# Tile 2 of a layer's token tiles in seven half-depth products of 256 tokens

## The chip, the cores and the metric

One core of a Trainium2 chip runs the program. The time of a run is what the device takes for one execution, in microseconds (us); a kernel's time is the median of its runs. The engines are TensorE (PE in the profile; its weight loads are PEld), VectorE (DVE), ScalarE (ACT) and GpSimd (POOL); SyncE (SP) issues the DMAs. Each engine takes its instructions in the order in which the program has them, and waits on semaphores where one needs what another engine wrote, or writes where another has still to read.

## What is computed

A retention layer over 2 batches of 768 tokens (8 heads of 64) gives x of 1536 tokens by 512. Two feed-forward layers follow, each 512 to 2048 to 512:

```python
def _moe_ref(x, w_in, w_out):
    h = x @ w_in
    g = np.maximum(h, 0.0) + np.log1p(np.exp(-np.abs(h)))
    return (g @ w_out).astype(np.float32)

def _moe2_ref(x, w_in, w_out, s, b):
    h = x @ w_in
    r = np.maximum(h, 0.0)
    g = s * (r * r) + b
    return (g @ w_out).astype(np.float32)
```

## The kernel before, in words

Tokens lie in three tiles of 512 (0, 1 and 2), the 2048 hidden units in 16 blocks of 128, in layer two taken as 8 pairs. The weights come as 64-bit numbers and are decoded on the chip (`split_w`: three VectorE steps and a ScalarE step make `wm`). Every operand of a product is kept in two parts, hi (`xh`, `wh`, `gh`) and lo (`xl`, `wl`, `gl`), and a product is three: hi by hi, hi by lo, lo by hi. ScalarE writes the hi part, GpSimd the lo part as the difference (`split`, L110 to L115; `parts_x`, L474).

The first matrix product of a layer takes a contraction of 512. `all_of` (L495) does it for one tile and block in 12 products of 512 columns. For tiles 0 and 1 of a pair together, the function `second` (L943) uses a scheme with seven products of half depth instead of eight: the 2 by 2 blocks are the halves of the contraction, the two weight blocks and the two tiles. Each of the seven is six products (`six`, L487). They use four sums of weights (`sums_w`, L306, on GpSimd; split into `sh`, `sl` by `split_sums`) and four sums of x (`sum_x`, L435; split into x1 to x4 once). Part results are kept by ScalarE copies out of the bank (`kept`, L502: p1, p5, u2) and added by VectorE (`joined`, L513). A product that adds on to a bank must come after the copy of what was there. The first pair of a layer goes without the scheme (`plain`, L915). Tile 2 is done by `all_of`, two times 12 products.

`begin`, `middle` and `finish` make g out of h: in layer two a relu out of the bank, a square, a scale with shift, and the hi part, all on ScalarE, then the lo part on GpSimd. The second matrix product is `acc_2` (12 products per tile and block); `take_2` (L580) brings its four banks to SBUF (`xa`) by four VectorE instructions of 512 columns, copies in the first pair, sums later.

The order is written out by hand. A pair in `second` has six slots. `part` starts the decode of one half of the next weights, `go_first` and `go_last` (L859 to L864) do steps of it ahead of and behind the second matrix product of the pair before, and `end_part` does its last step, the split. `pair` (L607) gives the order of the halves of a pair: (w, 0), (w + 1, 0), sums (w, 2), (w, 1), split of the sums (w, 3), (w + 1, 1). `load_w` (L269) issues the load of a half from SP into one of four buffers (`raw`); the decode of each half issues the load of a later one.

Layer two starts with `plain(1, 0, ...)` (L1068), in whose slots `all_x` makes the sums of x and `parts_x` splits them; then come seven pairs by `second`, and the last second products with the output.

Of the kernel before, what the change touches and what calls it, by code (L numbers as in the profile page):

```python
# [13 lines left out]
P = 128  # L14
# [34 lines left out]
def tile_retention_mlps(ctx: ExitStack, tc: tile.TileContext, head, w1, w2, sb, out):  # L49
    nc = tc.nc  # L50

    cp = ctx.enter_context(tc.tile_pool(name="cp", bufs=1))
    rawp = ctx.enter_context(tc.tile_pool(name="raw", bufs=4))
    dp = ctx.enter_context(tc.tile_pool(name="dec", bufs=2))
# [214 lines left out]
    def load_w(w, i):  # L269
        layer, f = divmod(w, NF)  # L270
        t = rawp.tile([P, DM, 2], U32, tag="raw", name="raw")
        nc.sync.dma_start(out=t.rearrange("p a b -> p (a b)"), in_=(w1, w2)[layer][f, :, i].bitcast(U32))
        raw_t[w, i] = t

    def split_w(w, i):
# [17 lines left out]
        nc.scalar.activation(m, hw.bitcast(F32), AF.Copy, scale=REBIAS)  # L293
        load_next()
        yield
# [205 lines left out]

    def kept(ps, tag):  # L502
        t = late.tile([P, TT], F32, tag=tag, name=tag)
        nc.scalar.activation(t, ps, AF.Copy)
        return t

    turn = [0]
# [5 lines left out]
    def joined(ps, t, here=False):  # L513
        c = ps if here else next_t()
        nc.vector.tensor_tensor(out=c, in0=ps, in1=t, op=ALU.add)  # L515
        return c
# [105 lines left out]
    at[1, PAIRS] = len(halves)  # L622
    RAWS = 4
# [92 lines left out]
    with tc.manual_schedule():  # L716
# [141 lines left out]

        def go_first():  # L859
            if work not in sums_of_w:  # L860
                go(work, 2)
# [81 lines left out]
        def second(la, p):  # L943
# [12 lines left out]

            part(base + 2)
            six(one, a11, b11, True)
# [3 lines left out]
            end_part()  # L962
            go_first()
# [5 lines left out]
            part(base + 3)  # L969
            six(other, s1, t1, True)  # L970
# [3 lines left out]
            end_part()  # L974
            go_first()
            whole(*of_pair(la, p - 1, 1, 1))
            go_last()

            part(base + 4)
            six(other, s4, b22, False)  # L980
# [3 lines left out]
            end_part()  # L984
            go_first()
            middle(c12)
# [5 lines left out]

            part(base + 5)
            six(one, a22, x_t[4], False)
            c21 = begin(la, one, tags=("u2", "p1"))
            end_part()
            go_first()
            whole(*of_pair(la, p - 1, 2, 1))
# [3 lines left out]

            part(base + 6)
            all_of(third, (ah, al), 2)
            ha = begin(la, third)
            end_part()
            go_first()
            middle(ha)
# [3 lines left out]

            part(base + 7)
# [4 lines left out]
            go_first()  # L1018
            middle(hb)
# [3 lines left out]
            finish(la, p, 1, 2, hb)  # L1023
            go_last()

        def all_x():
# [142 lines left out]
```

## Time and profile before

| | |
|---|---|
| runs | 567.87, 565.83, 565.73 us; median 565.83 |
| span of the profiled execution, from its first to its last instruction | 564.1 us |
| around the span, against the median | 1.7 us |
| TensorE busy | 559.1 us (99%), 2972 products |
| weight loads of TensorE busy | 461.8 us (82%) |
| VectorE busy | 368.0 us (65%) |
| ScalarE busy | 339.4 us (60%) |
| GpSimd busy | 340.9 us (60%) |
| loads of raw weights | 64 of 512 KB, 3.6 us from issue to landing |

The profile is one execution of the program. Busy time is the time in which an engine works at something; the chain that ended last goes back from the last instruction, at each step to what released it. A row of a timeline has the start in us from the span's start, the duration, the engine, the line of the code and the operation, what it writes and reads, and in brackets the idle time of the engine before it with what ended it. The durations of neighbouring instructions of an engine overlap somewhat, so the step from start to start says what one costs.

### The profile page before, as it was taken

Reading aid. Unit: us, or ns where it says so; the run is one execution under the profiler, and the core shown is the slowest. Engines: PE = TensorE matmul, PEld = TensorE weight load, DVE = VectorE, ACT = ScalarE, POOL = GpSimd, SP = SyncE. Lnnn points to the kernel's source line nnn. Section 1 sums busy time; section 2 is a strip of 40 time slices with the busy share of each in tenths; the row PEclk is TensorE's granted clock in tenths of the full one; section 3 lists DMA queues with packets and bytes.
Section 4 is the critical chain, followed back from the end, with each engine's and each line's share of the span. In section 5 each row is a group of like instructions: output and inputs, shape, how many; then the busy total and the mean of one; then the engine's idle time right before and its main releaser. Section 6 shows DMA issues by size and latency. Waiting matters only on the chain.

```text
span 564.1 us, 8073 instructions
## 1 busy us (share of the span) xinstructions
PE 559.1 (99%) x2972; PEld 461.8 (82%) x2972; DVE 368.0 (65%) x556; ACT 339.4 (60%) x616; POOL 340.9 (60%) x289
## 2 busy tenths in 40 slices
PE   8999999999999999999999999999999999999997
PEld 7877888888888888888888888888888888888886
DVE  4887768776757759786859865645645646544224
ACT  3766673544555665543437797768585966766560
POOL 4457467776598797733525996556565646556130
PEclk9999999999999999999999999999999999999999
DMA  8996211101222213322212022222122121100005
GB/s 341 407 355 223 74 42 56 57 19 59 74 76 74 76 37 112 110 79 78 67 43 76 21 92 75 76 73 67 47 76 74 59 92 37 38 0 2 0 4 220
DMA packets 15014, 50.58 MB, mean 90 GB/s; under 512 B 1792, under 2 KB 2048, under 8 KB 14976
## 3 DMA queue, kind: packets, MB, share of 16 engines
q1 hardware_dynamic: 14976, 50.08, 25.4%
q8 instruction: 23, 0.38, 0.3%
q14 instruction: 15, 0.12, 0.1%
HBM read 46.93 MB, written 3.15 MB: 89 GB/s over the span
## 4 chain that ended last, share of the span: by engine, by line
PE 97%; DVE 1%; DMA 1%; ACT 0%; issue 0%; DVEq 0%
PE acc L576 35%; PE acc L400 12%; PE h L490 10%; PE h L349 8%; PE y L498 7%; PE third L498 7%; PE y L490 5%; PE y L349 4%; PE third L490 2%; PE y L191 2%; PE h L498 2%; PE s L172 2%; PE h L191 1%; DMA qk<-head 1%; PE acc L172 1%; PE acc L191 1%
## 5 line engine op out<-in xcount | busy, mean ns | idle before, releaser
L586 DVE TENSOR_TENSOR xa<-acc,xa 128x512 f32<-128x512 f32 x131 | 81.7, 684 | 98.3 <-PE acc L576 98.1
L115 POOL TENSOR_TENSOR gl<-c,gh 128x512 fp32r<-128x512 f32 x69 | 91.8, 1334 | 83.0 <-ACT gh L112 65.0
L115 POOL TENSOR_TENSOR wl<-wm,wh 128x512 fp32r<-128x512 f32 x64 | 83.8, 1309 | 93.9 <-ACT wh L112 93.8
L576 PE MATMUL acc<-wh,gh 128*128 128x512 f32 x190 | 74.1, 390 | 0.0
L576 PE MATMUL acc<-wh,gl 128*128 128x512 f32 x190 | 73.9, 389 | 0.0
L576 PE MATMUL acc<-wl,gh 128*128 128x512 f32 x190 | 51.7, 389 | 0.0
L112 ACT ACTIVATE gh<-c 128x512 fp32r<-128x512 f32 x69 | 43.6, 632 | 11.1 <-POOL c L550 7.0
L297 DVE SCALAR_TENSOR_TENSOR wm<-wm,cu,word 128x512 uint32<-128x512 uint32 x54 | 40.1, 742 | 12.3 <-ACT wm L293 11.5
L293 ACT ACTIVATE wm<-raw 128x512 f32<-128x512 f32 x64 | 42.1, 658 | 7.1 <-POOL wl L115 7.0
L576 PEld LDWEIGHTS acc<-wh,gh 128*128 128x128 f32 x190 | 35.7, 188 | 8.2 <-DVE xa L586 0.4
L290 DVE SCALAR_TENSOR_TENSOR word<-raw,cu,word 128x512 uint32<-128x512 uint32 x54 | 40.8, 756 | 1.9
L576 PEld LDWEIGHTS acc<-wl,gh 128*128 128x128 f32 x190 | 35.7, 188 | 7.5
L576 PEld LDWEIGHTS acc<-wh,gl 128*128 128x128 f32 x190 | 35.7, 188 | 7.3
L112 ACT ACTIVATE wh<-wm 128x512 fp32r<-128x512 f32 x64 | 39.7, 620 | 3.1 <-DVE wm L297 3.0
L548 ACT ACTIVATE c<-c,sbt 128x512 f32<-128x512 f32 x48 | 39.2, 817 | 1.6
L362 ACT ACTIVATE t<-t 128x512 f32<-128x512 f32 x24 | 15.1, 628 | 39.0 <-DVE t L356 39.0
L400 PE MATMUL acc<-gh,wh 128*128 128x512 f32 x96 | 37.9, 395 | 0.0
L522 ACT ACTIVATE c<-c 128x512 f32<-128x512 f32 x21 | 13.3, 632 | 40.5 <-DVE c L515 39.9
L400 PE MATMUL acc<-gl,wh 128*128 128x512 f32 x96 | 37.4, 390 | 0.0
L288 DVE TENSOR_SCALAR word<-raw 128x512 uint32<-128x512 uint32 x54 | 37.1, 687 | 0.5
L576 PE MATMUL acc<-gh,wh 128*128 128x512 f32 x96 | 37.3, 389 | 0.0
L576 PE MATMUL acc<-gl,wh 128*128 128x512 f32 x96 | 37.3, 389 | 0.0
(240 smaller groups left out, 1390.7 us busy)
## 6 DMA issues: line engine op xcount, KB each, us to landing
raw<-w SPq DMA_DIRECT2D x64, 512.0 KB, 3.6
qk<-head SPq DMA_DIRECT2D x12, 512.0 KB, 8.4
kv<-head SPq DMA_DIRECT2D x12, 512.0 KB, 8.4
out<-xa SPq DMA_DIRECT2D x11, 256.0 KB, 2.1
cst<-head SPq DMA_DIRECT2D x1, 518.0 KB, 4.5
cst<-head SPq DMA_DIRECT2D x1, 256.0 KB, 5.5
out<-xa SPq DMA_DIRECT2D x2, 128.0 KB, 1.8
sbt<-sb SPq DMA_DIRECT2D x1, 1.0 KB, 10.2
```

The costliest lines, as they stand in the source:

```text
L112: nc.scalar.activation(hi, src, AF.Copy)
L115: lo_eng.tensor_tensor(out=lo, in0=src, in1=hi.bitcast(F32), op=ALU.subtract)
L290: nc.vector.scalar_tensor_tensor(out=x, in0=hw, scalar=cu[:, 0:1], in1=x, op0=ALU.bitwise_and, op1=ALU.bitwise_or)
L293: nc.scalar.activation(m, hw.bitcast(F32), AF.Copy, scale=REBIAS)
L297: nc.vector.scalar_tensor_tensor(out=m.bitcast(U32), in0=m.bitcast(U32), scalar=cu[:, 1:2], in1=x, op0=ALU.logical_shift_left, op1=ALU.bit ...
L349: nc.tensor.matmul(ps, w[:, cc * P : (cc + 1) * P], r[j][:, cc, :], start=i == 0, stop=i == len(ops) - 1)
L400: nc.tensor.matmul(acc_t[la, g, j][cc], *ops[i], start=f4 == 0 and i == 0, stop=ends(s) and i == 2)
L490: nc.tensor.matmul(ps, w[a][:, k * P : (k + 1) * P], x[b][:, k], start=start and i == 0, stop=i == len(ops) - 1, skip_group_check=True,)
L498: nc.tensor.matmul(ps, w[a][:, k * P : (k + 1) * P], (xh, xl)[b][j][:, k], start=i == 0, stop=i == len(ops) - 1)
L548: nc.scalar.activation(c, c, AF.Identity, scale=sbt[:, 0:1], bias=sbt[:, 1:2])
L576: nc.tensor.matmul(acc_t[la, p, "pair", j][cc], *ops[i], start=half == 0 and i == 0, stop=half == 1 and i == 2)
L586: nc.vector.tensor_tensor(out=dst, in0=ps, in1=dst, op=ALU.add)
```

## The change

Tile 2 goes into the scheme as well, from the second pair of layer two on. Its 512 tokens are cut into two halves of 256 (`LEFT`, `RIGHT`), which play the part that tiles 0 and 1 play; the sums of weights are those of the pair already. `last_tile` replaces the last two slots of `second` in layer two: seven times six products of 256 columns, with copies and sums of 256 columns, among them the second products of tile 0 in halves of two banks (`FIRST`, `SECOND`).

The scheme needs four sums of x of tile 2, z1 to z4, made once (`sum_z`, `parts_z`): nine VectorE instructions of 512 elements over hi and lo parts, in `all_z` in the last two slots of `plain`, four hi parts on ScalarE and four lo parts on GpSimd; z4 is split in the last slot of `plain`, z1 to z3 in the first two slots of the first `second`. They live in `xa[2]`, and split in places of `xh`, `xl` that are free by then, z4 in buffers of its own. To make room for those the raw buffers of the weights become three, with a fourth in a pool that ends with the retention layer.

The sums of weights are needed to the end of a pair now. So their split moves to the last slot of the pair before, everything in the decode of layer two comes one slot later (`- la`), and the four GpSimd sums are done at the head of their slot (`go_first(la)`).

```diff
-    rawp = ctx.enter_context(tc.tile_pool(name="raw", bufs=4))
+    rawp = ctx.enter_context(tc.tile_pool(name="raw", bufs=3))
...
     def load_w(w, i):
         layer, f = divmod(w, NF)
-        t = rawp.tile([P, DM, 2], U32, tag="raw", name="raw")
+        k = halves.index((w, i))
+        pool, more = (rp, {"tag": "raw_"}) if k in FOURTH else (rawp, {"tag": "raw"})
+        t = pool.tile([P, DM, 2], U32, name="raw", **more)
...
-        load_next()
+        if halves.index((w, i)) != FOURTH[-1]:
+            load_next()
...
+    def room_z(k):
+
+        if k < 3:
+            return [wide(t[1][:, k - 1]) for t in (xh, xl)]
+        if k == 3:
+            return [t[2][:, 0:2, RIGHT] for t in (xh, xl)]
+        return [late.tile([P, 2, HT], F32R, tag=f"z{e}", name=f"z{e}") for e in "hl"]
+
+    def sum_z(ks):
+
+        def of(half, cols):
+            return [t[2][:, 2 * half : 2 * half + 2, cols].bitcast(F32) for t in (xh, xl)]
+
+        add, less = ALU.add, ALU.subtract
+        (h11, l11), (h12, l12), (h21, l21), (h22, l22) = (of(a, b) for a in (0, 1) for b in (LEFT, RIGHT))
+        z1, z2 = raw_z(1), raw_z(2)
+        todo = {
+            1: ((h12, h11, less), (None, l12, add), (None, l11, less)),
+            2: ((h22, z1, less), (None, l22, add)),
+            3: ((z2, h11, less), (None, l11, less)),
+            4: ((h21, z2, less), (None, l21, add)),
+        }
+        for k in ks:
+            for x, y, op in todo[k]:
+                nc.vector.tensor_tensor(out=raw_z(k), in0=raw_z(k) if x is None else x, in1=y, op=op)
+
+    def parts_z(k):
+        z_t[k] = hi, lo = room_z(k)
+        split(hi, lo, raw_z(k), nc.scalar, nc.gpsimd)
...
-            return [(w, 0), (w + 1, 0), (w, 2)] + [(w, 1), (w, 3)][:: 1 if la else -1] + [(w + 1, 1)]
+            return [(w, 0), (w + 1, 0), (w, 2)] + [[(w, 3), (w, 1), (w + 1, 1)], [(w, 1), (w + 1, 1), (w, 3)]][la]
...
+    FOURTH = 3, 7
...
-        def go_first():
-            if work not in sums_of_w:
+        def go_first(la):
+            if work not in sums_of_w or la and len(sums_of_w) % 2:
                 go(work, 2)
...
-            part(base + 2)
+            part(base + 2 - la)
...
+            if la and p == 1:
+                parts_z(1)
...
+            if la and p == 1:
+                parts_z(2)
+                parts_z(3)
...
+            if la:
+                last_tile(la, p, base, third, (a11, a12, a22), (s1, s2, s3, s4))
+                return
...
+        def last_tile(la, p, base, third, a, sums):
+
+            (a11, a12, a22), (s1, s2, s3, s4) = a, sums
+            q11, q21, q22 = (
+                [t[2][:, 2 * k : 2 * k + 2, cols] for t in (xh, xl)] for k, cols in ((0, LEFT), (1, LEFT), (1, RIGHT))
+            )
+            z1, z2, z3, z4 = (z_t[k] for k in (1, 2, 3, 4))
+
+            part(base + 6 - la)
+            other = bank(ps_y, "y")
+            u, v, w_, x = other[:, LEFT], other[:, RIGHT], third[:, LEFT], third[:, RIGHT]
+            six(u, a11, q11, True)
+            p1 = kept(u, "p1", HT)
+            six(w_, a12, q21, True)
+            six(x, s1, z1, True)
+            p5 = kept(x, "p5", HT)
+            joined(w_, p1, True)
+            end_part()
+            go_first(la)
+            acc_2(la, p, 0, 0, FIRST)
+            six(u, s2, z2, False)
+            u2 = kept(u, "u2", HT)
+            six(x, s4, q22, False)
+            joined(x, u2, True)
+            ha = begin(la, third)
+            acc_2(la, p, 0, 0, SECOND)
+            finish(la, p, 0, 2, ha)
+            go_last()
+
+            part(base + 7 - la)
+            six(u, s3, z3, False)
+            joined(u, p5, to=v)
+            end_part()
+            go_first(la)
+            acc_2(la, p, 0, 1, FIRST)
+            take_2(la, p, 0, FIRST)
+            six(u, a22, z4, False)
+            hb = begin(la, other)
+            acc_2(la, p, 0, 1, SECOND)
+            take_2(la, p, 0, SECOND)
+            finish(la, p, 1, 2, hb)
+            go_last()
+
+        def all_z():
+            sum_z((1, 2))
+            yield
+            sum_z((3, 4))
+            parts_z(4)
+            yield
...
-        plain(1, 0, left, [[sums_1], [sums_1], [], [sums_1], [], []], [(1,), (3, 2), (), (4,), (), ()])
+        sums_z = all_z()
+        plain(1, 0, left, [[sums_1], [sums_1], [], [sums_1], [sums_z], [sums_z]], [(1,), (3, 2), (), (4,), (), ()])
```

Where instructions stand now is seen best in the built programs. Lines of the changed kernel are shifted: L293 before is L295 now, L297 is L300, L481 is L484, L504 is L507, L515 is L558, L522, L547 and L548 are L565, L590 and L591. First ScalarE late in layer two's `plain`, before, from a split of weights to tile 2's relu, square, scale and hi part for the first block (`sh` is the hi part of the sums of weights, `x4h` that of x's fourth sum):

```order
L112 ACTIVATE wh_3184<-wm 128x512
L112 ACTIVATE sh<-ws 128x512 x2
L481 ACTIVATE x4h<-xa_110 128x1024
L522 ACTIVATE c<-third 128x512
L547 ACTIVATE c<-c 128x512
L548 ACTIVATE c<-c,sbt 128x512
L112 ACTIVATE gh<-c 128x512
```

The same stretch now:

```order
L112 ACTIVATE wh_3182<-wm 128x512
L295 ACTIVATE wm<-raw 128x512
L484 ACTIVATE x4h<-xa_110 128x1024
L565 ACTIVATE c<-third 128x512
L590 ACTIVATE c<-c 128x512
L591 ACTIVATE c<-c,sbt 128x512
L112 ACTIVATE gh<-c 128x512
L112 ACTIVATE wh_3229<-wm 128x512
L112 ACTIVATE sh<-ws 128x512 x2
```

A decode's `wm` stands where `sh` stood, and `sh` comes behind the tile and one more split.

Next ScalarE at the end of `plain`, before, up to the first copy of the first `second` pair (`p_3328<-h`; `c<-y` begins tile 2's second block):

```order
L522 ACTIVATE c<-y 128x512
L547 ACTIVATE c<-c 128x512
L548 ACTIVATE c<-c,sbt 128x512
L112 ACTIVATE gh<-c 128x512
L112 ACTIVATE wh_3279<-wm 128x512
L293 ACTIVATE wm<-raw 128x512
L504 ACTIVATE p_3328<-h 128x512
```

And now (`zh` is the hi part of z4, `p_3339<-h` the first copy):

```order
L565 ACTIVATE c<-y 128x512
L590 ACTIVATE c<-c 128x512
L591 ACTIVATE c<-c,sbt 128x512
L112 ACTIVATE gh<-c 128x512
L295 ACTIVATE wm<-raw 128x512
L112 ACTIVATE zh<-xa_111 128x512
L507 ACTIVATE p_3339<-h 128x512
```

`zh` has come between the last `wm` and the first copy.

VectorE at the same place, before, from tile 0's copies out of the banks (`xa_109<-acc`, L584) over two decodes to the join that reads the first copy:

```order
L584 COPY xa_109<-acc_3216 128x512 x2
L584 COPY xa_109<-acc_3217 128x512
L584 COPY xa_109<-acc_3218 128x512
L288 TENSOR_SCALAR word<-raw 128x512
L290 SCALAR_TENSOR_TENSOR word<-raw,cu,word 128x512
L297 SCALAR_TENSOR_TENSOR wm<-wm,cu,word 128x512
L288 TENSOR_SCALAR word<-raw 128x512
L290 SCALAR_TENSOR_TENSOR word<-raw,cu,word 128x512
L297 SCALAR_TENSOR_TENSOR wm<-wm,cu,word 128x512
L515 TENSOR_TENSOR c<-third,p_3328 128x512
```

VectorE there now, behind the same copies, with the sums z1 to z4 (L544):

```order
L544 TENSOR_TENSOR xa_111<-xh_105 128x512
L544 TENSOR_TENSOR xa_111<-xa_111,xl_108 128x512 x2
L544 TENSOR_TENSOR xa_111<-xh_105,xa_111 128x512
L544 TENSOR_TENSOR xa_111<-xa_111,xl_108 128x512
L290 TENSOR_SCALAR word<-raw 128x512
L292 SCALAR_TENSOR_TENSOR word<-raw,cu,word 128x512
L300 SCALAR_TENSOR_TENSOR wm<-wm,cu,word 128x512
L544 TENSOR_TENSOR xa_111<-xa_111,xh_105 128x512
L544 TENSOR_TENSOR xa_111<-xa_111,xl_108 128x512
L544 TENSOR_TENSOR xa_111<-xh_105,xa_111 128x512
L544 TENSOR_TENSOR xa_111<-xa_111,xl_108 128x512
L558 TENSOR_TENSOR c<-third,p_3339 128x512
```

One decode (three instructions) has stayed ahead of the join out of two, and nine sums have come in, five ahead of that decode and four behind it.

## Rows read from the trace of the kernel before

**Rows 1.** The page: busy us, share, count; then shares of the last chain.
```profile
PE 559.1 (99%) x2972; PEld 461.8 (82%) x2972; DVE 368.0 (65%) x556; ACT 339.4 (60%) x616; POOL 340.9 (60%) x289
...
PE 97%; DVE 1%; DMA 1%; ACT 0%; issue 0%; DVEq 0%
```

**Rows 2.** The last chain in time: start, us, engine, tile, line, count.
```profile
330.67 1.36 PE h L490 x6
...
361.95 1.36 PE h L490 x6
```

**Rows 3.** Busy us by engine in one pair; then clock, DMA share, GB/s.
```profile
361.95:393.23 31.28, 31.28 (x140) 25.90 (x139) 17.86 (x28) 22.31 (x38) 18.28 (x16) 1.00 0.21 68
```

**Rows 4.** Timeline of TensorE at the tail, first and last of twelve.
```profile
559.31 0.28 PE L1087 MATMUL acc<-wh,gh 128*128 128x256 f32 x1
...
560.62 0.28 PE L1087 MATMUL h<-wl,gh 128*128 128x256 f32 x1
```

**Rows 5.** Timeline of TensorE in pair 1, and in a later pair.
```profile
337.31 0.39 PE L490 MATMUL h<-x2h,sh 128*128 128x512 f32 x1
...
507.31 0.39 PE L498 MATMUL third<-xh,wh 128*128 128x512 f32 x1
```

**Rows 6.** Timeline of ScalarE in that later pair.
```profile
509.10 0.63 ACT L112 ACTIVATE gh<-c 128x512 fp32r<-128x512 f32 x1
```

**Rows 7.** Groups of ScalarE: busy, mean ns, idle before.
```profile
L223 ACT ACTIVATE xh<-y 128x256 fp32r<-128x256 f32 x13 | 4.8, 372 | 2.3 <-PE y L191 2.3
```

**Rows 8.** Timeline of ScalarE at the end of layer two's first pair.
```profile
324.83 0.62 ACT L112 ACTIVATE wh<-wm 128x512 fp32r<-128x512 f32 x1
325.35 1.14 ACT L112 ACTIVATE sh<-ws 128x512 fp32r<-128x512 f32 x2
326.39 1.04 ACT L481 ACTIVATE x4h<-xa 128x1024 fp32r<-128x1024 f32 x1
327.34 0.58 ACT L522 ACTIVATE c<-third 128x512 f32<-128x512 f32 x1
...
330.00 0.66 ACT L293 ACTIVATE wm<-raw 128x512 f32<-128x512 f32 x1
...
334.47 0.58 ACT L504 ACTIVATE p<-h 128x512 f32<-128x512 f32 x1
```

**Rows 9.** Timeline of GpSimd in layer one, and by pair 1 of two.
```profile
106.76 1.73 POOL L386 TENSOR_TENSOR gl<-t,gh 128x512 fp32r<-128x512 f32 x1
111.57 1.29 POOL L386 TENSOR_TENSOR gl<-t,gh 128x512 fp32r<-128x512 f32 x1 [3.08 <-ACT gh L382]
...
330.78 2.54 POOL L484 TENSOR_TENSOR x4l<-xa,x4h 128x512 fp32r<-128x512 f32 x2
```

**Rows 10.** Timeline of VectorE at the end of layer two's first pair.
```profile
322.95 1.68 DVE L444 TENSOR_TENSOR xa<-xa,xa 128x1024 f32<-128x1024 f32 x1
327.54 2.48 DVE L584 COPY xa<-acc 128x512 f32<-128x512 f32 x4 [2.91 <-PE acc L576]
329.94 0.69 DVE L288 TENSOR_SCALAR word<-raw 128x512 uint32<-128x512 uint32 x1
...
332.33 0.69 DVE L288 TENSOR_SCALAR word<-raw 128x512 uint32<-128x512 uint32 x1
```

**Rows 11.** Timeline of VectorE in layer one, sums over SBUF.
```profile
107.27 1.77 DVE L461 TENSOR_TENSOR p<-p,xl 128x512 f32<-128x512 f32 x1
108.97 0.68 DVE L461 TENSOR_TENSOR u<-u,xl 128x512 f32<-128x512 f32 x1
```

**Rows 12.** Windows about TensorE's last product, columns as in rows 3.
```profile
558.00:560.70 2.70, 2.70 (x19) 2.46 (x17) 2.40 (x4) 0.00 (x0) 0.00 (x0) 1.00 0.43 159
...
563.40:564.10 0.70, 0.00 (x0) 0.00 (x0) 0.00 (x0) 0.00 (x0) 0.00 (x0) 0.50 0.00 0
```

**Rows 13.** Timeline of TensorE in the first ten microseconds.
```profile
4.45 1.23 PE L172 MATMUL s<-qk 64*128 64x128 f32 x8
...
8.98 0.71 PE L172 MATMUL s<-qk 64*128 64x128 f32 x8
```

More of the change, by code (lines that the diff above doesn't have):

```diff
@@ L500, in all_of, with kept, wide, raw_z @@
             )
-    def kept(ps, tag):
-        t = late.tile([P, TT], F32, tag=tag, name=tag)
+    def kept(ps, tag, cols=TT):
+        t = late.tile([P, TT], F32, tag=tag, name=tag)[:, :cols]
         nc.scalar.activation(t, ps, AF.Copy)
         return t
+    LEFT, RIGHT = slice(0, TT // 2), slice(TT // 2, TT)
+    HT = TT // 2
+    z_t = {}
+    def wide(t):
+        return t.rearrange("p (a t) -> p a t", a=2)
+    def raw_z(k):
+        return wide(xa[2][:, k - 1])
+    def room_z(k):
[22 more added lines that the diff above has]
+        split(hi, lo, raw_z(k), nc.scalar, nc.gpsimd)
     turn = [0]
@@ L511, in next_t, with joined @@
         return tp.tile([P, TT], F32, tag="t2" if turn[0] else "t1", name="c")
-    def joined(ps, t, here=False):
-        c = ps if here else next_t()
+    def joined(ps, t, here=False, to=None):
+        c = to if to is not None else ps if here else next_t()
         nc.vector.tensor_tensor(out=c, in0=ps, in1=t, op=ALU.add)
@@ L622, in tile_retention_mlps @@
     at[1, PAIRS] = len(halves)
-    RAWS = 4
+    FOURTH = 3, 7
     loads, splits = iter([x for x in halves if x[1] < 2]), iter(halves)
@@ L962, in second @@
             end_part()
-            go_first()
+            go_first(la)
             middle(c11)
@@ L967, in second @@
             go_last()
-            part(base + 3)
+            if la and p == 1:
+                parts_z(1)
+            part(base + 3 - la)
             six(other, s1, t1, True)
@@ L974, in second @@
             end_part()
-            go_first()
+            go_first(la)
             whole(*of_pair(la, p - 1, 1, 1))
             go_last()
-            part(base + 4)
+            if la and p == 1:
+                parts_z(2)
+                parts_z(3)
+            part(base + 4 - la)
             six(other, s4, b22, False)
@@ L984, in second @@
             end_part()
-            go_first()
+            go_first(la)
             middle(c12)
@@ L991, in second @@
             go_last()
-            part(base + 5)
+            part(base + 5 - la)
             six(one, a22, x_t[4], False)
@@ L996, in second @@
             end_part()
-            go_first()
+            go_first(la)
             whole(*of_pair(la, p - 1, 2, 1))
@@ L1001, in second @@
             go_last()
-            part(base + 6)
+            if la:
+                last_tile(la, p, base, third, (a11, a12, a22), (s1, s2, s3, s4))
+                return
+            part(base + 6 - la)
             all_of(third, (ah, al), 2)
@@ L1006, in second @@
             end_part()
-            go_first()
+            go_first(la)
             middle(ha)
@@ L1011, in second @@
             go_last()
-            part(base + 7)
+            part(base + 7 - la)
             other = bank(ps_y, "y")
@@ L1017, in second @@
             end_part()
-            go_first()
+            go_first(la)
             middle(hb)
@@ L1024, in second @@
             go_last()
+        def last_tile(la, p, base, third, a, sums):
[4 more added lines that the diff above has]
+            z1, z2, z3, z4 = (z_t[k] for k in (1, 2, 3, 4))
+            part(base + 6 - la)
+            other = bank(ps_y, "y")
[7 more added lines that the diff above has]
+            end_part()
+            go_first(la)
+            acc_2(la, p, 0, 0, FIRST)
[7 more added lines that the diff above has]
+            go_last()
+            part(base + 7 - la)
+            six(u, s3, z3, False)
+            joined(u, p5, to=v)
+            end_part()
+            go_first(la)
+            acc_2(la, p, 0, 1, FIRST)
[12 more added lines that the diff above has]
+            yield
         def all_x():
```

## The prediction

> **What bounds the kernel now.** I read the shares of busy time first. TensorE is busy 99% of the span, and the chain that ended last is TensorE for 97% of its length [rows 1]: no other engine decides, except where it makes TensorE wait. The chain in order of time then gives the unit of layer two: a pair of weight blocks that begins at 330.67 is followed by the next at 361.95, 31.28 us later [rows 2]. I count 138 products of 512 columns in a pair (42 of tiles 0 and 1, 24 of tile 2, 72 of the second matrices), so one costs 31.28 / 138 = 0.2267 us, and twelve cost the 2.72 us that the chain's rows show. In such a pair TensorE is busy 31.28 of 31.28 us [rows 3]: there is no gap that something could fall into, and each product that goes is worth its whole pace. By the same token each wait that is put in costs its whole length. ScalarE is busy 22.31 us of the pair, VectorE 17.86, GpSimd 18.28 [rows 3]: all have room on average, so what has to be looked at is their order, not their load.
>
> **The products.** In each of seven pairs 24 products of 512 columns become 42 of 256. The trace holds twelve products of that shape with another stationary operand each time, in the tail: the first starts at 559.31, the last at 560.62, eleven steps of 0.1191 us [rows 4]. That is a little over half of 0.2267, so halving the width costs about 0.006 us a product. Per pair: 24 x 0.2267 - 42 x 0.1191 = 5.441 - 5.002 = 0.439 us; seven pairs give **-3.07 us**. Beside this row stands a rule: the Trainium skill, page "TensorE: Matmul & The Clock Gate", section "Wait — 56ns, not 53.3ns?", has a fixed cost of some 2.5 ns a product beside the columns over 2.4 GHz. By it a pair would save an estimated 24 x 0.2158 - 42 x 0.1092 = 0.59 us and seven 4.2; the rows show more per product than that, and the sum goes by them.
>
> **The steady pairs.** New in each pair are three copies of 256 columns on ScalarE and three sums of 256 columns on VectorE, and weights' splits change places. They pass if each reader is in time. The tightest place is the first copy (P1 of tile 2), which must be done before `six(u, s2, z2, False)` adds to the same bank. Before, tile 2's first product starts at 507.31 [rows 5] and ScalarE is through with the work ahead of that copy (the hi part of c21) at 509.10 + 0.63 less its overlap, about 509.7, that is 2.4 us later [rows 6]. A 256-column read of a bank costs it 0.37 us [rows 7], so the copy ends some 2.8 us after tile 2's first product. TensorE asks for it after three products of six (2.15) and six of the second matrix (1.36): 3.5 us. Spare: 0.7 us, so **0**; were that cover gone, a tenth of a microsecond short in each of the other six pairs would cost 0.6 in all. The sums of weights are split in the last slot now. Their first half follows hb's chain: ScalarE some 2.66 (relu to hi, as in [rows 8] from 327.34 to 330.00), GpSimd 1.30 for gl and 1.27 for sl ([rows 9]: two in 2.54), begun 1.36 before the pair's end, ready 3.9 us into the next pair and needed there at 5.44. Priced at 0 too. The third buffer for raw weights: a load lands while three halves are split, one in a slot of at least 4 us, and no engine waits for one in the pairs shown; SP's queue holds only these loads there. Zero.
>
> **The first pair.** Here lies the cost. Nine new VectorE sums (`sum_z`) stand behind tile 0's four copies out of PSUM, with three instructions of a weight's split between the fifth and the sixth. ScalarE's new `zh` reads the last of them, and directly behind `zh` in ScalarE's order stands the copy p1 of the pair's first product, which before came with nothing but weights ahead of it, at 334.47 [rows 8]. TensorE needs p1 at 337.31, when h<-x2h adds to that bank [rows 5]. So TensorE now waits for the whole chain of sums. I walk it.
> - ScalarE's `wm` of pair 1's last half now comes where `sh` came, at 325.35 [rows 8], and ends at 326.0. VectorE's `wm` and then `sum_x(4)` follow: 326.7 + 1.68 [rows 10] = 328.4. Tile 0's four copies, 2.40 before the next starts [rows 10], bring it to **330.8**.
> - ScalarE, held up by `sum_x(4)`, does x4h by 329.4, then relu to hi of one tile 2.66, a `wh` 0.52 (324.83 to 325.35), two `sh` 1.04 (325.35 to 326.39), the next relu to hi 2.7, and ends the first `wm` of pair 2 near 337.0.
> - GpSimd from 329.4 on: two x4l, gl, wl, two sl, gl, each 1.27 alone [rows 9]: busy beyond 338 without a gap.
> - What does a VectorE sum with both inputs in SBUF cost beside GpSimd? One of layer one's sums took 1.77, with the next 1.70 after it, while GpSimd's own went from 1.27 to 1.73; the next took 0.68, in the 3.08 us in which GpSimd stood idle [rows 9, 11]. The five sums of `sum_z((1, 2))` meet GpSimd busy: the first ends with the running GpSimd instruction near 332.4, four more at 1.70: **339.2**. The three instructions of the split take 332.33 - 329.94 = 2.4 with a short wait among them [rows 10], 2.2 without: 341.4. By then GpSimd has nothing to do (its next, zl, waits for `zh`), so the last four take some 0.65 each: **344.0**.
> - `zh` 0.5 and p1 0.6: **345.1**. TensorE stands from 337.31: **+7.8 us**.
> Bounds: were no sum slowed, the five would end at 334.1, but the split's `wm` waits for ScalarE's 337.0, so 337.7, 340.3 and 341.4: 4.1 us. Were the last four slowed as well, 348.2 and 349.3: 12.0. I take 7.8, since the slowed rows are of the same instruction, shape and neighbours; I see no reason for the upper end.
>
> **After the wait.** ScalarE is late for the next copy too: relu of c11 behind VectorE's join (345.8), wh, square, scale, hi, z1's hi and p5 end at about 350.1; TensorE at full pace would ask for it at 345.1 + 1.36 + 2.72 = 349.2: 0.9 us more. But TensorE may not be at full pace. Its granted clock is 1.00 in the window up to 560.70 and 0.50 (1.2 of 2.4 GHz) in that from 563.40, less than 3 us after its last product [rows 12]; and after the idle start of the program eight L172 products take 1.23 us at 4.45 and 0.71 at 8.98 [rows 13]. So a standstill of 7.8 us should end at the lower level. The first product is at 1.45, and by 8.98 the pace is full: at half pace for some 4 to 5 us TensorE loses 2 to 2.5, and the 0.9 hides in that. Between 0.9 and 2.5 I take **+2.0**. A rule stands beside these rows: the Trainium skill, the same page, section "HAM oscillation — how this bites in real kernels", says that a wait for data between bursts throttles the array, so that the next burst starts cold. By it the 2.0 is due and 0.9 is not an end. Nothing later is short: z1 to z3 are split by about 354 and tile 2 begins near 360.
>
> **Sum.** 564.1 (profiled span) - 3.07 + 7.8 + 2.0 = 570.8. The median of the runs, 565.83, lies 1.7 above the span, for what lies around it: **572.5 us**, +1.2%.
>
> **Rivals.**
> - The sums run at full speed beside GpSimd, the chain's lower end. For: the new access pattern is two rows of 256 instead of one of 512, and no row shows it. Against: [rows 11]. The wait is 4.1, the clock may still fall: 565.83 - 3.07 + 4.1 + 0 to 2 = 566.9 to 568.9, which is no change to the eye.
> - The gain stays: the chain of sums is done before p1 is needed. This is the faster side. It decides at 337.31 less 1.1 for `zh` and p1: VectorE would have to end `sum_z(4)` by 336.2, but tile 0's copies cannot end before 329.94 [rows 10], and nine sums and three instructions at their fastest (0.6 and 0.7) are 7.6 more, 337.5. Only if ScalarE's rows and mine were off together. Time 562.8.
> - More waits than I see: the last four sums slowed too (+4.2), or the 0.7 us spare of the steady pairs is not there (0.5 in each of six, +3): 575.5 to 577.
> - That the products are not cheaper at all (0.1295 a product of 256 would end the gain) I rule out by [rows 4].
>
> **Chances.** The forecast's case, 570 to 575: 0.70. Full-speed sums: 0.14. Gain kept: 0.06. More waits: 0.10. The range leaves out the second rival and most of the third: 567.0 to 575.0. About 0.5% (2.8 us) is what a measurement of this kernel can tell from no change, so faster means under 563.0 and slower over 568.7. Faster: half of the gain kept and a little besides, 0.05. Same: most of the full-speed case and the rest of the gain kept, 0.16. Slower: 0.79.
>
> **What would show it.** Right: a pair of 30.84 us from the second on; 256-column products 0.119 apart; in the first pair a standstill of TensorE ahead of h<-x2h that ScalarE's p1 ends, `zh` ahead of p1 waiting for a VectorE `sum_z`, five sums of 1.7 and four of 0.7; products at 0.43 behind it. Wrong: `zh` done by 336.5, or no gap ahead of h<-x2h; waits in every pair ahead of the 256-column products would mean that the spare of 0.7 was mine alone.

## The result and the profile after

The changed kernel takes 572.25 us (571.99 to 572.53), the kernel before, run beside it, 565.88 us: 1.0109 times as long, interval 1.0092 to 1.0126. The forecast was 572.5, in a range of 567.0 to 575.0. The profiled execution lasts 571.99 us with a span of 570.2, against a span of 564.1 before.

The page has TensorE at 98% of a longer span with less to do, and the chain that ended last is no longer TensorE's alone: VectorE now holds 4% of it, where it had 1% [rows 1]. Busy us, share, count; then the shares of the chain:

```profile
PE 558.6 (98%) x3098; PEld 466.5 (82%) x3098; DVE 385.6 (68%) x586; ACT 348.7 (61%) x641; POOL 346.7 (61%) x293
...
PE 93%; DVE 4%; ACT 2%; issue 1%; DVEq 0%
```

The chain in order of time says where those shares lie, and answers to [rows 2]. Start, us, engine, tile, line, count:

```profile
334.87 1.68 DVE xa L544
336.58 1.64 DVE xa L544
344.38 2.93 PE h L493 x6
...
370.42 1.36 PE h L493 x6
...
401.38 1.36 PE h L493 x6
```

From 370.42 on a pair follows the last after 30.96 us, and so do all up to the tail; before it was 31.28. So the products did become cheaper. All that was lost, and more, was lost in pair 1, about 344.38, where the chain comes to TensorE from VectorE's L544, the line of `sum_z`. Pair 1, by the starts of its first product and of pair 2's, took 40.01 us. The timeline of TensorE shows the two places (start, us, what; in brackets the idle time before, and what ended it):

```profile
336.37 0.39 PE L493 MATMUL y<-x1l,sh 128*128 128x512 f32 x1
337.72 0.73 PE L493 MATMUL y<-x1h,sl 128*128 128x512 f32 x2 [0.97 <-POOL sl L115]
344.38 0.80 PE L493 MATMUL h<-x2h,sh 128*128 128x512 f32 x1 [5.92 <-ACT p L507]
344.97 0.63 PE L493 MATMUL h<-x2l,sh 128*128 128x512 f32 x1
345.40 0.63 PE L493 MATMUL h<-x2h,sh 128*128 128x512 f32 x1
```

One wait of about 1 us for the low part of the sums of weights, one of about 6 for the copy p1, and behind it products 0.43 us apart instead of 0.2267. The windows over that wait, and over the products behind it, show the granted clock: 0.50, the lower of its two levels (1.2 of 2.4 GHz), and 0.53, after 1.00 before (us; then busy us and count of TensorE, its loads, VectorE, ScalarE, GpSimd; then clock, DMA share, GB/s). The third window is a steady pair and answers to [rows 3]: no gap in TensorE.

```profile
341.40:344.30 2.90, 0.00 (x0) 0.00 (x0) 1.74 (x3) 1.09 (x2) 0.38 (x1) 0.50 0.28 112
344.40:348.10 3.70, 3.70 (x9) 2.98 (x10) 2.01 (x3) 2.95 (x5) 2.07 (x2) 0.53 0.02 4
...
370.26:401.22 30.96, 30.96 (x157) 26.42 (x156) 18.89 (x31) 23.37 (x41) 18.17 (x17) 1.00 0.20 68
```

ScalarE's timeline has the link between the two: `zh` waits for VectorE's last sum, and p1 comes right behind it.

```profile
343.21 0.63 ACT L112 ACTIVATE zh<-xa 128x512 fp32r<-128x512 f32 x1 [6.27 <-DVE xa L544]
343.75 0.58 ACT L507 ACTIVATE p<-h 128x512 f32<-128x512 f32 x1
```

VectorE's timeline says why the sums were so late. It answers to [rows 10]; the nine sums are the rows of L544 (of the last four the first and the last are shown):

```profile
328.32 2.47 DVE L627 COPY xa<-acc 128x512 f32<-128x512 f32 x4
330.72 0.71 DVE L544 TENSOR_TENSOR xa<-xh 128x512 f32<-128x512 f32 x1
331.46 3.38 DVE L544 TENSOR_TENSOR xa<-xa,xl 128x512 f32<-128x512 f32 x2
334.87 1.67 DVE L544 TENSOR_TENSOR xa<-xh,xa 128x512 f32<-128x512 f32 x1
336.58 1.64 DVE L544 TENSOR_TENSOR xa<-xa,xl 128x512 f32<-128x512 f32 x1
...
339.72 0.75 DVE L300 SCALAR_TENSOR_TENSOR wm<-wm,cu,word 128x512 uint32<-128x512 uint32 x1
340.39 0.74 DVE L544 TENSOR_TENSOR xa<-xa,xh 128x512 f32<-128x512 f32 x1
...
342.49 0.69 DVE L544 TENSOR_TENSOR xa<-xa,xl 128x512 f32<-128x512 f32 x1
```

Four sums at 1.64 to 1.69, then four at 0.68 to 0.74: the same instruction, with GpSimd busy beside the first group and idle from 340.57 on. GpSimd pays too: it did `wl` in 1.75 and the two `sl` in 3.40, where one takes 1.27 alone, and that is why the first `sl` came 1.1 us late for TensorE (asked for at 336.60):

```profile
334.24 1.75 POOL L115 TENSOR_TENSOR wl<-wm,wh 128x512 fp32r<-128x512 f32 x1
335.95 3.40 POOL L115 TENSOR_TENSOR sl<-ws,sh 128x512 fp32r<-128x512 f32 x2
339.31 1.26 POOL L115 TENSOR_TENSOR gl<-c,gh 128x512 fp32r<-128x512 f32 x1
343.92 1.28 POOL L115 TENSOR_TENSOR zl<-xa,zh 128x512 fp32r<-128x512 f32 x1 [3.34 <-ACT zh L112]
```

The GPSIMD Engine Reference of the Trainium skill, section "Key points", has GpSimd share its SBUF interfaces with VectorE and contend with VectorE instructions of two SBUF inputs. The rows agree, with 0.69 against 1.67 on VectorE and 1.27 against 1.75 on GpSimd. A VectorE sum that takes one input from a bank of TensorE's results, as L629 does, keeps its pace beside GpSimd: its 131 instructions take 0.68 on average, and the 75 with GpSimd at work throughout take at most 0.69.

### The profile page after: what moved, and what is told of

The parts are those of the page before. It is cut to its first block, busy times and chain, and to the rows that moved or that the text cites. A ratio compares the mean times of both kernels' runs of the same rounds, so it can differ in the third digit from the quotient of the medians.

```text
span 570.2 us, 8406 instructions
## 1 busy us (share of the span) xinstructions
PE 558.6 (98%) x3098; PEld 466.5 (82%) x3098; DVE 385.6 (68%) x586; ACT 348.7 (61%) x641; POOL 346.7 (61%) x293
## 2 busy tenths in 40 slices
DMA packets 15016, 50.61 MB, mean 89 GB/s; under 512 B 1792, under 2 KB 2048, under 8 KB 14976
## 4 chain that ended last, share of the span: by engine, by line
PE 93%; DVE 4%; ACT 2%; issue 1%; DVEq 0%
PE acc L619 33%; PE acc L403 11%; PE h L493 10%; PE y L493 8%; PE h L352 8%; PE third L493 5%; PE y L352 4%; PE third L501 3%; PE y L501 3%; PE y L191 2%; DVE xa L544 2%; PE s L172 2%; PE h L501 1%; PE h L191 1%; PE acc L780 1%; PE acc L172 1%
## 5 line engine op out<-in xcount | busy, mean ns | idle before, releaser
L629 DVE TENSOR_TENSOR xa<-acc,xa 128x512 f32<-128x512 f32 x131 | 82.4, 684 | 71.2 <-PE acc L619 71.0
L619 PE MATMUL acc<-wl,gh 128*128 128x512 f32 x190 | 53.9, 390 | 0.0
L295 ACT ACTIVATE wm<-raw 128x512 f32<-128x512 f32 x64 | 42.4, 662 | 7.1 <-POOL wl L115 7.0
L300 DVE SCALAR_TENSOR_TENSOR wm<-wm,cu,word 128x512 uint32<-128x512 uint32 x54 | 40.0, 740 | 4.6 <-ACT wm L295 4.0
L591 ACT ACTIVATE c<-c,sbt 128x512 f32<-128x512 f32 x48 | 39.2, 816 | 1.6
L565 ACT ACTIVATE c<-c 128x512 f32<-128x512 f32 x21 | 13.1, 633 | 35.1 <-DVE c L558 35.1
```

Source lines behind the costliest of these rows:

```text
L300: nc.vector.scalar_tensor_tensor(out=m.bitcast(U32), in0=m.bitcast(U32), scalar=cu[:, 1:2], in1=x, op0=ALU.logical_shift_left, op1=ALU.bit ...
L591: nc.scalar.activation(c, c, AF.Identity, scale=sbt[:, 0:1], bias=sbt[:, 1:2])
L619: nc.tensor.matmul(acc_t[la, p, "pair", j][cc], *ops[i], start=half == 0 and i == 0, stop=half == 1 and i == 2)
L629: nc.vector.tensor_tensor(out=dst, in0=ps, in1=dst, op=ALU.add)
```

## The experiments

All are made from the changed kernel, except the one on columns. "Pair 1" is the time from its first product to pair 2's in the profiled execution, which in e8 and e9 was 1.1 to 1.2 us quicker than the median; in all of them a later pair takes 30.96.

| kernel | us, median | of before (interval) | pair 1 | mean clock in the profile |
|---|---|---|---|---|
| changed | 572.25 | 1.0109 (1.0092 to 1.0126) | 40.01 | 0.994 |
| e1 no sums | 565.08 | 0.9989 (0.9980 to 0.9997) | 32.90 | 1.000 |
| e2 zh late | 572.84 | 1.0127 (1.0112 to 1.0142) | 40.28 | 0.994 |
| e3 kept warm | 571.36 | 1.0099 (1.0086 to 1.0112) | 39.30 | 1.000 |
| e4 five sums, spread | 569.32 | 1.0054 (1.0039 to 1.0069) | 37.55 | 0.994 |
| e5 low parts on VectorE | 564.14 | 0.9971 (0.9960 to 0.9982) | 31.97 | 0.999 |
| e6 z1 later | 563.71 | 0.9958 (0.9946 to 0.9970) | 31.59 | 1.000 |
| e8 count alone | 571.03 | 1.0089 (1.0076 to 1.0102) | 37.81 | 0.994 |
| e9 places alone | 568.32 | 1.0043 (1.0029 to 1.0057) | 34.80 | 1.000 |

**Is it the sums?** e1 leaves them out, and nothing else:

```diff
     def sum_z(ks):
         ...
-        for k in ks:
-            for x, y, op in todo[k]:
-                ...
+        return
```

> The changed kernel without the nine VectorE sums that make z1 to z4 (sum_z does nothing; the splits zh, zl read whatever lies in xa[2]). Theory (the sums, through zh and the copy p1 behind it, make the whole loss; the seven pairs save 0.32 us each, as 30.96 against 31.28 us in the traces): 565.9 - 2.2 = 563.6 us, no standstill of TensorE ahead of h<-x2h, a pair of 30.96 us. Rival A (the 256-column products and the extra copies lose time on their own): no better than 566. Rival B (zh, zl and the later split of the weights' sums already make TensorE wait in the first pair): 564.5 to 567 with a gap ahead of y<-x1h,sl.

It took 565.08: the sums cost 7.2 us, and the clock stayed at 1.00. But it is 1.5 above what the theory gave, and within rival B's range, though the wait is not where rival B had it. TensorE's waits, us in total, times and longest, say why:

```profile
PE h L493 <- ACT p L507: 0.8, 1, 0.8
PE y L493 <- ACT p L507: 0.6, 1, 0.6
```

Both are pair 1's copies, p1 and p5. ScalarE had been held up 2.67 us by `sum_x(4)`, which the changed order puts behind a decode, and `zh`, 0.52 us, still stood ahead of p1. So a wait for p1 was there without any sum, as the forecast's walk of ScalarE's order had it (free near 337.0, then `zh` and p1, against 337.31), only hidden behind the sums. VectorE's timeline of e1 shows the room there was for them, idle times of 4.8, 2.0 and 4.3 us in pair 1:

```profile
337.20 0.75 DVE L300 SCALAR_TENSOR_TENSOR wm<-wm,cu,word 128x512 uint32<-128x512 uint32 x1 [4.79 <-ACT wm L295]
...
342.27 2.48 DVE L625 COPY xa<-acc 128x512 f32<-128x512 f32 x4 [1.99 <-PE acc L617]
...
352.65 2.48 DVE L625 COPY xa<-acc 128x512 f32<-128x512 f32 x4 [4.33 <-PE acc L617]
```

**Is it the place of `zh`?** e2 moves z4's parts to where z1's are, so that p1 no longer stands behind them:

```diff
             sum_z((3, 4))
-            parts_z(4)
 ...
             if la and p == 1:
                 parts_z(1)
+                parts_z(4)
```

> z4 is split behind c11 in the first slot of pair 1 (where z1 is split) instead of ahead of it, so the copy p1 no longer stands behind zh; nothing else changes. Theory (VectorE's sums are the load, and whatever stands behind them waits): p1 is done near 337.5, but the join of c11 stays at 343.2 behind the nine sums, relu of c11, a split, square, scale, gh, two z parts and then p5 follow on ScalarE, p5 ends near 348.6 and TensorE stands ahead of y<-xh,sh from 341 to 348.6, then at half pace: 571 to 573 us in all, no real change. Rival (the place of zh alone makes the wait): the wait goes, 563 to 565 us.

p1 was done at 337.5, and the time did not move. TensorE simply waited at the next copy. The wait, and ScalarE's rows of p1, the relu and p5:

```profile
PE y L493 <- ACT p L507: 6.0, 1, 6.0
...
336.89 0.58 ACT L507 ACTIVATE p<-h 128x512 f32<-128x512 f32 x1
343.89 0.63 ACT L565 ACTIVATE c<-c 128x512 f32<-128x512 f32 x1 [6.42 <-DVE c L558]
...
348.01 0.58 ACT L507 ACTIVATE p<-y 128x512 f32<-128x512 f32 x1
```

The join of c11 (L558) stands behind the sums on VectorE, ScalarE's relu behind the join, and p5 behind that. VectorE's queue is the cause; ScalarE's order only chooses the place of the wait.

**What does the clock cost?** e3 repeats the six products ahead of the wait five times in pair 1, so that TensorE has something to do; each repeat overwrites the last:

```diff
-            six(other, s1, t1, True)
+            for _ in range(5 if la and p == 1 else 1):
+                six(other, s1, t1, True)
```

> In pair 1 the first product of slot two (six products of y<-x1h) is done five times over instead of once, into the same bank with the same result, so that TensorE works while it waits for p1. Theory (the fall of the clock costs 1.7 us and hides 0.8 us of ScalarE's late p5): the granted clock stays 1.00, h<-x2h starts at 344.4 as before and goes at 0.227 a product, y<-xh,sh then waits for p5 until 349.3 against 350.18 now: 0.9 us less, 571.4 us. Rival A (the clock costs the whole 1.7 and p5 is in time): 570.5. Rival B (the clock costs nothing on the path): 572.25.

571.36, as expected. The product that waits for p1 still came at 344.48, but the next followed 0.34 us behind it and the one after that 0.23, at a clock of 1.00; p5 then was late by 0.7. So of the 1.72 us that the eight slow products of the changed kernel had cost (steps of 0.594 to 0.381 instead of 0.2267), 0.7 came back by pair 1's length and 0.9 by the medians. The rest had covered p5, and the first products behind each of the two waits, which are slow at full clock as well (0.34).

**Fewer sums, in other places.** e4 makes x once (high plus low part, 2048 wide) and each z from it in one sum, and puts them where VectorE has room: x and z1 in pair 0's last slot but one, z2 behind the first join of pair 1, z3 and z4 behind the last join of tile 1, with their high parts on VectorE. `sum_x(4)` goes ahead of the decode that the change had put before it. The lines of the new `sum_z` and of `sum_x(4)` are left out here.

```diff
...
             go_last()
             if la and p == 1:
-                parts_z(1)
+                sum_z((2,))
...
             if la and p == 1:
+                parts_z(1)
                 parts_z(2)
-                parts_z(3)
...
             finish(la, p, 1, 1, c22)
             go_last()
+            if la and p == 1:
+                sum_z((3, 4))
+                parts_z(3, nc.vector)
+                parts_z(4, nc.vector)
...
         def all_z():
-            sum_z((1, 2))
-            yield
-            sum_z((3, 4))
-            parts_z(4)
+            sum_z((0, 1))
             yield
```

> The same products, with the work for z1 to z4 done otherwise: hi plus lo of all of tile 2 in one VectorE instruction of 2048 elements, then four sums of 512 in place, five instructions for nine; the first two in plain's fifth slot, z2 behind the join of c11, z3 and z4 (hi parts on VectorE) behind the join of c22; the fourth sum of x of tiles 0 and 1 one step earlier, as before. Theory (the loss is VectorE's queue at the start of pair 1): p1 near 335.2 and p5 near 341, standstill under 1 us, 563.5 to 564.7 us, faster than both kernels. Rival (ScalarE or GpSimd cannot take the z parts in pair 1): a wait at the copies or the takes of tile 2 there, 566 to 570.

A miss by 5 us, and in the rival's range: the wait for p1 was gone, and another of 3.3 us stood at 353.4, at the takes of tile 2, with a half clock behind it. VectorE's and GpSimd's timelines name it:

```profile
355.53 1.29 DVE L621 COPY xa<-acc 128x512 f32<-128x512 f32 x2 [5.19 <-POOL xl L115]
```
```profile
354.22 1.28 POOL L115 TENSOR_TENSOR xl<-xa,xh 128x512 fp32r<-128x512 f32 x1
355.44 1.28 POOL L115 TENSOR_TENSOR zl<-xa,zh 128x512 fp32r<-128x512 f32 x1
```

The raw sums stand in `xa[2]`, and pair 1's `take_2` of tile 2 writes its output to `xa[2]`. So the take waited until GpSimd had read z3, behind four sums of weights and two `gl`, and TensorE waited for the take's banks. I had looked for readers of the sums, and not for the next writer of their room.

**That wait taken away.** e5 gives the low parts of z3 and z4 to VectorE as well; nothing else differs from e4:

```diff
-        split(hi, lo, raw_z(k), eng or nc.scalar, nc.gpsimd)
+        split(hi, lo, raw_z(k), eng or nc.scalar, eng or nc.gpsimd)
```

> The five-sum kernel (569.32 us) with one edit: the low parts of z3 and z4 are taken by VectorE right behind their high parts, not by GpSimd behind the sums of weights. Theory: in the five-sum kernel nothing is wrong with the sums; its one long wait in pair 1 (3.50 us between two starts at 353.37, then about 1.7 us of half clock) is a take of tile 2 that writes the block of SBUF in which z3 and z4 stand raw, and so had to wait for GpSimd's low parts (done 356.7). Without that: 569.32 - 3.3 - 1.7 = 564.3 us, clock 1.000, no step over 0.6 us in pair 1. Rival A: VectorE's two low parts (0.7 us each, 1.7 beside GpSimd) push the same take back by 1.4 to 3.4 us, so a wait of 1 to 3 us stays: 565.3 to 568. Rival B: the wait there is for something else (banks of sums, weights): 568 to 569.3.

564.14, 0.2 under the expectation, at full clock. e6 moves z1's sum from pair 0 to beside z2's:

```diff
-            sum_z((0, 1))
+            sum_z((0,))
 ...
-                sum_z((2,))
+                sum_z((1, 2))
```

> The kernel with low parts on VectorE, and z1's sum moved from pair 0's last slot to beside z2's, behind the first join of pair 1. Theory: the 0.28 us that TensorE waits for the low part of the sums of weights at 336.9 comes from GpSimd running slower beside VectorE's sums (its 1.29 us subtract took 3.34 and the next 1.75 in the five-sum kernel); with z1 out of the way the second is 1.29 again and the wait goes: 564.3 - 0.3 = 564.0 us. The floor by the steady pairs is 565.88 - 7 x 0.32 = 563.6. Rival: z1 and z2 now stand ahead of the copies of tile 1 (about 1.4 us idle there) and push the joins of pair 1 back: 564.8 to 566.

563.71, 0.3 under, and the wait for `sl` is gone; of TensorE's waits these are left (the first is at the program's start, the last ahead of layer two, so layer two has only the second):

```profile
PE acc L774 <- DVE xa L756: 1.4, 1, 1.4
PE acc L613 <- DVE xa L621: 0.2, 1, 0.2
PE h L352 <- DVE xl L229: 0.2, 1, 0.2
```

This version is quicker than both kernels, 2.2 us under before (0.9958, 0.9946 to 0.9970). e5 and e6 are not told apart by their intervals, but by pair 1's length, 31.97 and 31.59.

**Count or place?** e8 has e4's five sums in the places of the changed kernel; e9 has the changed kernel's nine sums in the places of e6.

```diff
 e8, from the changed kernel, with e4's sum_z:
-            sum_z((1, 2))
+            sum_z((0, 1, 2))
 e9, from e6, with the changed kernel's sum_z:
-            sum_z((0,))
+            sum_z((1,))
 ...
-                sum_z((1, 2))
+                sum_z((2,))
```

> The changed kernel with five sums (one of 2048 wide, four of 512) instead of nine, in the same places of the order, z1 and z2 in pair 0's last slot but one, z3, z4 and z4's parts in its last. Theory (the place does most of the harm, since TensorE's first product with x2 waits behind everything VectorE does up to the last sum): VectorE's sums would run 330.7 to 337.1 (3.0 + 1.67 + 1.67), its decode to 339.3, z3 and z4 to 340.7, then 0.6 for z4's high part and 0.5 for p1: the product starts at 341.9, not 344.4, a wait of 3.8 us that still brings the half clock (a 3.5 us wait did, one of 1.2 did not). 572.25 - 2.5 = 569.8 us, clock 0.994. Rival A (count): with four sums fewer the wait shrinks to about 1 us and the clock holds: 565 to 566.5. Rival B: the sums run at a price by width, the total is the same as of nine: 571.5 to 572.5.

> The changed kernel's nine sums (three, two, two and two) in the places of the quickest kernel so far (563.71 us): z1's in pair 0's last slot but one, z2's behind the first join of pair 1, z3's and z4's with all their parts on VectorE behind the last join of tile 1, and the last sum of x ahead of the decode. Theory (place): the sums of z1 and z2 fit VectorE's idle time there, z3's and z4's two further sums (0.65 us each, GpSimd idle) push decode and the copies of tile 2 back by 1.3 us, and TensorE's short wait at 353.1 grows by that: 563.7 + 1.4 = 565.1 us, 565.4 if the low part of the sums of weights is late again; clock 1.000. Rival A (count): nine sums bring a wait of over 3 us and the half clock wherever they stand: 568 to 572. Rival B: VectorE has room for them behind the join too: 563.6 to 564.2.

e8 took 571.03 (569.88 to 571.51; the profiled run 569.92), where 569.8 was expected, rival A had 565 to 566.5 and rival B 571.5 to 572.5. The one wait of 3.8 us that was expected came as two, of the same kind as the changed kernel's:

```profile
PE h L493 <- ACT p L507: 2.2, 1, 2.2
PE y L493 <- POOL sl L115: 2.1, 1, 2.1
```

e9 took 568.32, 3.2 over the expectation and in the range of its rival A. Its runs lie between 566.87 with a mean clock of 1.000 and 569.72 with 0.994, so whether the clock fell behind its one wait differed from run to run. The wait is 3.34 us, not 1.6:

```profile
356.87 0.50 PE L619 MATMUL acc<-wh,gh 128*128 128x512 f32 x1 [3.34 <-DVE xa L627]
```
```profile
347.78 0.69 DVE L544 TENSOR_TENSOR xa<-xh,xa 128x512 f32<-128x512 f32 x1
348.50 1.67 DVE L544 TENSOR_TENSOR xa<-xa,xl 128x512 f32<-128x512 f32 x1
350.09 0.96 DVE L114 CAST xh<-xa 128x512 fp32r<-128x512 f32 x1
```

I had reckoned with an idle GpSimd at all four sums. By the fourth it was at work again (from 347.80), and that sum took 1.67, the casts behind it 0.96, where e4 has one of 0.42 at 347.10, and each step behind them was late. So neither count nor place alone is the cause: in the old places four sums fewer bring 1.2 us, in the new ones 4.6; and the new places bring 3.9 with nine sums, 7.3 with five. "New places" here takes in `sum_x(4)` ahead of the decode and the parts of z3 and z4 on VectorE; no run has these by themselves. That they count is seen from e1: without any sum, but with `sum_x(4)` and `zh` where the change had put them, it takes 1.4 us more than e6 with its five.

**The price of a product.** e7 puts 96 products whose results are overwritten into each of pairs 1 to 6 of the kernel before:

```diff
+            bench(other, s1, t1, BENCH.get(p, ()) if la else ())
             six(other, s1, t1, True)
```

> The kernel before, with 96 idle products put ahead of the first product with a sum of weights in each of pairs 1 to 6 (their results are overwritten; nothing else is changed): pair 1 six of 256 columns and six of 512, eight times over; pair 2 48 of 256, then 48 of 512; pair 3 256 and 512 by turns; pair 4 twelve and twelve, four times; pair 5 48 of 128, then 48 of 512; pair 6 48 of 384, then 48 of 512. Theory (the edge costs): a block of 256 goes at 0.120 us a step whatever runs beside it, and the first six 512s behind it take 0.028 us more than 1.360; pair 1's 96 then take 16.9 us or a little over, pair 2's 16.65 (one edge). Rival A (neighbours cost): the slow 512s of the changed kernel come from what the other engines do there; here, with those engines waiting, 512s behind 256s step at 0.2267 and pair 1 and pair 2 take the same within 0.05 us. Rival B (columns and a fixed part): from 256 at 0.120 and 512 at 0.2267 a step is 0.0133 + 0.000417 a column, so 128 gives 0.067 and 384 0.173 us; against that a floor by the loading of the stationary operand, with which 128 columns would take about 0.11 to 0.12 as 256 do.

The one run took 668.41 us. The 96 products took 16.80, 16.66, 16.96, 16.72, 16.30 and 19.27 us in pairs 1 to 6; pairs 1 and 2 are 0.14 apart, where rival A had them the same within 0.05. Rows of pair 1 (a block of six of 256, a block of six of 512, the next block):

```profile
335.77 0.28 PE L500 MATMUL y<-x1h,sh 128*128 128x256 f32 x1
...
336.48 0.40 PE L500 MATMUL y<-x1h,sh 128*128 128x512 f32 x1
336.71 0.40 PE L500 MATMUL y<-x1l,sh 128*128 128x512 f32 x1
...
337.87 0.28 PE L500 MATMUL y<-x1h,sh 128*128 128x256 f32 x1
```

The block of 512 takes 1.39, not 1.36. In nanoseconds from start to start, worked out from the records of pair 2, at the change from 256 to 512 columns:

```
... 120 120 120 119 | 234 236 228 232 232 226 227 226 227 227 226 ...
```

The first five 512s behind a 256 are slower, 28 ns together, and then the pace is back, and in the window 388.50 to 391.50 about that change no engine but TensorE was busy: the edge costs, not the neighbours. Nor does it need narrower products ahead: behind a wait the 512s go through the same steps (e1 from 338.55 on: 235, 233, 236, 224, 231, 236). What makes the edge is open. The same happens behind 384 columns (42 ns over nine steps) and behind 128 (about 110 ns over ten, the first at 292). And 384 columns step at 0.1735, 256 at 0.120, 512 at 0.2267: a fixed 13.3 ns and 0.417 ns a column fit all three. 128 columns go at 0.112, not at the 0.067 of that line: a floor. The Trainium skill, page "TensorE: Matmul & The Clock Gate", section "LDWEIGHTS (loading the stationary operand)", gives a load of P columns P / 1.2 ns, for 128 columns an estimated 0.107 us; that the floor is this load is my reading. Each of the 96 products has a load of its own, and no run here left loads out to show it.

## Why the prediction was right

**What bounds the kernel.** Right, and the lengths add up. Span before 564.11; pair 1 began 0.26 earlier; pair 1 was 9.05 longer than 30.96; six steps from pair to pair saved 0.32 each; from pair 7's start to the end 45.09 instead of 45.92. 564.11 - 0.26 + 9.05 - 1.92 - 0.83 = 570.15.

**The products: the mis-sized term.** The forecast was 0.439 a pair and 3.07 in all; measured were 0.32 a pair, 2.24 for seven. The step that failed took the tail's 0.1191 [rows 4] for the whole price. The 42 products do take 5.01 us (forecast 5.00). But each pair has four blocks of 256 columns with 512s behind them, and those six 512s take 1.388 instead of 1.360: 0.11 a pair. In the tail's rows no 512 follows. e7 shows that edge on its own. The chain has it too, as the groups of six that take 1.39. The total hid the miss of 0.83 by luck. Pair 1's wait and half clock came to 9.05, where 9.8 was forecast. 0.30 came from a stall of TensorE's at 549.2 that the kernel before had and the changed one has not, 0.19 from the stretch behind the last product and 0.26 from pair 1's earlier start, none of which I had forecast; the stretch from pair 7 on lasts 45.92 in e7's trace of the kernel before as well, while pair 1's start lies anywhere from 330.25 to 330.67 in the eleven traces. What sets either is open.

**The rule on the fixed cost.** The 2.5 ns a product of the Trainium skill ("TensorE: Matmul & The Clock Gate", section "Wait — 56ns, not 53.3ns?") would have made it an estimated 4.2 us for seven pairs. The runs show 13.3 ns and 2.24 us, so rows and not rule were the right price, and e7 the better row.

**Steady pairs: zero.** Right: pairs 2 to 6 take 30.960 each, within 0.001, and pair 7 has no wait. The spare at the first copy was 0.36 us (copy done 424.80, asked for at 425.16), half of the 0.7 forecast.

**The first pair.** Right in mechanism and place, step by step: copies of tile 0 done at 330.7 (forecast 330.8), five sums by 338.2 (339.2; the first took 0.71, not 1.7, while GpSimd's instruction beside it grew instead), split by 340.5 (341.4), last four by 343.2 (344.0), `zh` and p1 by 344.3 (345.1). TensorE would have asked at 337.05 and started at 344.38: 7.3 against 7.8. What I had not seen is the second victim of the same contention: `sl`, the low part of the sums of weights, which I walked at GpSimd's pace alone and did not hold against TensorE's need of it (336.86 in the kernel before, 336.60 now). It cost nothing only because p1 was later still. In e4 and e5 it shows as 0.3, in e8 as 2.1.

**After the wait.** 1.72 at half clock against 2.0, with p5's lateness hidden in it, as written; e3 shows both parts. The forecast leant on the slow products at the program's start; the profile does not show the clock low there (the window 0.50 to 6.80 reads 1.00), so those rows show a pace and no level of the clock. Behind the wait of 6 us the clock fell in every run of the changed kernel; behind the one of 3.3 (e4, e9) it fell in some runs and not in others (e4: 570.25 at a mean clock of 0.994, 567.41 at 1.000); behind those of 0.8 and 0.6 (e1) it did not. The length of the wait alone does not tell: in e8's profiled run the clock was at 0.50 from 338.90 to 339.90, right behind the wait of 2.1, and in e9's it was at 1.00 behind 3.34. The rule of the Trainium skill that the forecast named, that a wait for data lets the next burst start cold ("TensorE: Matmul & The Clock Gate", section "HAM oscillation — how this bites in real kernels"), agrees with the changed kernel's 6 us.

**Rivals.** The sums at full speed fell by the rows at 1.67; "more waits" fell by the steady pairs; the kept gain fell here, but e6 shows that it was to be had, 563.7, with other places for fewer sums. I had asked whether the sums as written could be done in time, and not where else VectorE had room.

## What to carry to other kernels

A one-time preparation that saves a little in each later step has to be walked through the queue of each engine that issues it, up to the first instruction behind it that the bounding engine waits for: here nine instructions on an engine that was busy 65% cost 7.2 us (e1), where seven pairs of cheaper products gave 2.2. Moving the waited-for copy out of the way (e2) does nothing where the next one stands behind the same queue; spreading the work over the idle places and making it shorter does, and each needs the other (e8, e9). And whoever parks data in a buffer looks for its next writer as well as for its readers (e4).

## What the runs showed that was not expected

- A product of 512 columns behind one of fewer is slower for five to ten steps: 28 ns in all behind 256, 42 behind 384, about 110 behind 128. Behind a wait the same slow steps follow the first product, with no narrower one ahead (e1, e3).
- Products of 128 columns, each with its own load of a stationary operand, step at 0.112 us, hardly under the 0.120 of 256: two of them cost 0.224, where one of 256 costs 0.120.
- The first product behind a wait steps 0.335 us at full clock instead of 0.227 (e1 at 338.22, e3 at 344.48, e9 at 356.87): each such wait costs 0.11 more than its length.
- The granted clock fell behind a wait of 2.1 us in one profiled run (e8) and stayed at 1.00 behind one of 3.34 in another (e9).
- Two engines in contention do not share the loss evenly: beside one sum of 2048 columns (3.0 us) GpSimd's `gl` took 3.34 instead of 1.27 (e4, e6), while beside the changed kernel's first sum (0.71) two `x4l` took 3.01 instead of 2.54.
